# An attention and long-convolution kernel: the convolution kernel's spectrum from a table of matmuls instead of an expanded table and an FFT, and one order list for the whole program

## The chip, the cores and the metric

The kernel runs on one core of a Trainium2 chip. A core has five engines with an instruction queue each: TensorE (PE; the load of its weights is shown as PEld), VectorE (DVE), ScalarE (ACT), GpSimd (POOL) and SyncE (SP, which here only issues DMAs). Work passes from one to the other through semaphores. The metric is the device time of one execution in microseconds, lower is better.

## The reference, cut to what matters

```python
x = A_x                                        # bf16, 1 x 2048 x 640
g = sigmoid((x * gate_w).sum(-1))              # one gate for each position
a = attention(x, wqkv, wo)                     # 32 heads of 20, each position sees 8 positions, 2 apart
b = ssm(x, A, B, C, log_dt, Dskip)
out = g * a + (1 - g) * b

def ssm(u, ...):                               # 640 channels, 192 complex states each
    l = arange(2048).astype(bfloat16)
    P = exp(dt * A * l)                        # 640 x 192 x 2048, complex
    K = einsum("dn,dnl,dn->dl", C, P, dt * B).real
    y = irfft(rfft(pad(u, 4096)) * rfft(pad(K, 4096)))[:2048]     # causal convolution along the positions
    return y + u * Dskip
```

The positions `l` are rounded to bf16, so of 2048 positions only 641 are distinct: 0 to 256, then steps of 2, 4 and 8. The convolution kernel K has 641 different values for each channel, repeated over the positions that round to the same number.

## The kernel before

The host part of the program adds tasks with a name, an engine, dependences and buffer slots to a `Plan`; a list of numbers (`SEQ1`, later `SEQ2`) gives the order in which the tasks are emitted. The tasks of an engine run in that order. A letter behind a number says which of ScalarE (A) and VectorE (D) does an eviction that either could do. The data flows in these steps:

- **Start** (`Attn.loads`, `Attn.window`, `SSMParams.build`). x is loaded in four quarters and transposed on TensorE (tasks `turn`, line L200; evictions `tev`). The parameter chain, passes over 128x960 values on VectorE and ScalarE from `wr` (L582) to the last subtraction (L615), turns A, B, C and dt into pieces of phases and logarithms. They go to DRAM (`Sprm`) and come back as matmul weights (`L`, line L720).
- **Attention** (`Attn.plan_late`, `plan_core`). Projections of 512 positions (`late`, L291, evictions `lev`); products of q and k on VectorE (`prod`, L350); sums over a head on TensorE (L356); maximum (`mx`, L370) and normalisation (`at`, L391); products with v (`pv`, L419); sums (`gat`, L425) with evictions `oT`; output projection (`wo`, L443); gated result (`ga`) into DRAM (`gaS`).
- **Kernel values** (`KGen.plan`). Ten chunks of channels. In each, matmuls on `L` (L747) give arguments, ScalarE takes sines (L759) and exponentials (L761), VectorE multiplies them (`pt`, `qq`, L782 to L784) and TensorE sums over the states (`kmm`, L800, weights of 32 columns). The two factors span 32 positions in steps of 8 and 22 offsets; `fin` (L1214) copies a chunk's sums to `E`.
- **Expansion** (`KExpand`), after five chunks each. VectorE copies the entries of `E` to all 2048 positions (`X`, L846), the result goes to DRAM (`Kx`) and comes back with other rows (`kc`).
- **FFT of 4096 points as 32 x 64.** `first` does the first step (L1231) for K (`f1`, `fk`, from `kc`) and the input (`fu`, from `Usb`) in tasks of eight matmuls, with evictions of 128x1024 (L469 on ScalarE, L471 on VectorE).
- **Second list** (`fft_conv`). Eight blocks of frequencies. For K and the input, real and imaginary part, one task each (`fp`, L1008, PHI of 128 columns as weights, real and imaginary inputs as two accumulating matmuls), evicted on ScalarE (`sp_k`, `sp_u`, 128x1280); on VectorE the complex product (L1041, sums L1044) into `Y`. Then the inverse: first step (L1069, evictions `cp`), last step with psi as weights (`yp`, L1097), and the mix with the gated attention result `gaF` (L1103, L1106, L1110), stored from L1122 on. `PHI` (384 KB for each block), `psi` and `gaF` are loaded bit by bit, each behind a small copy that waits for an eviction.

The line that evicts a block of the spectrum, and the product, before:

```python
evict(nc, en, spec[nm, ro][:], fp[:, :, 0:320].rearrange("p f x -> p x f"))          # 128 x 320 x 4
nc.vector.tensor_tensor(t[o][:, 4*x0:4*x1], spec[i0][:, 4*x0:4*x1], spec[i1][:, 4*x0:4*x1], ALU.mult)
nc.vector.tensor_tensor(yv[:, ro, 4*x0:4*x1, 4*fb:4*fb + 4], t[f"ta{ro}"][...], t["tc"][...], (ALU.subtract, ALU.add)[ro])
```

Of the kernel before, what the change touches and what calls it, by code (L numbers as in the profile page):

```python
# [20 lines left out]
S = 2048  # L21
D = 640
# [14 lines left out]
def _attn_consts():  # L37
# [7 lines left out]
    for wp in range(W):  # L45
# [3 lines left out]

PLAN = dict(free=dict(P=4.0, A=4.2, D=4.7, S=16.0, G=16.0), phase=0.0, ms=-562.9, kg=3.6, wl=2678.4, look=0.3, ba=-39.4, bd=-694.1, grace=2227.4, p0=-605.9, p1=7.4,  # L50
            tx=[1831.6, 2062.6], txw=316.4, ql=-639.9, vl=-579.1, pw=39.8, el=-872.0, tl=303.3, vw=170.4, gate=1159.7,
            l=[985.4, 547.2, 222.2, 579.5, 238.7, 662.0, 1153.9, 985.5, 777.6, 1276.6, 963.9, 1335.9],
            a=[-383.8, 509.3, -1088.5, -67.5, 191.2, 725.6, 1205.9, 786.5], v=[1509.9, 971.2, 1675.0, 1085.1, 2426.4, 1181.7, 871.1, 1340.5],
            g=[102.8, 729.6, -565.5, -597.5, -1036.3, -403.5, 622.8, -317.4, -275.5, -968.3, -775.7],
            dl=[157.8, 67.2, 403.1, 10.3, -181.3, 324.5, 197.3, 230.9, 179.6, -259.4],
            kl=[-437.0, -232.8, -303.6, -188.9, -840.1, 140.8, -865.3, -73.8, -172.8, -518.6], Ll=2038.2, argl=332.8, xl=787.7, c0=5667.4, x0=-271.9, x1=332.2,
            f0=-509.9, f1=247.7, u0=1630.4, u1=60.1, off={0: 260.3, 9: 345.9, 27: 254.6, 47: 93.4, 96: -22.0, 105: -27.0, 107: 4.7, 131: -28.8, 140: -41.5,
            142: 18.2, 145: -3.0, 146: -3.7, 149: -9.3, 151: -10.5, 155: -2.9, 166: -1.8, 173: 5.1, 193: -12.8, 197: -5.4, 208: 10.3, 210: -36.0, 218: -30.6,
            1004: -8.8, 1022: -37.2, 1083: 6.1, 1089: 5.2, 1099: -2.5})


SEQ1 = """
8 0 2 3 1 6 4 14 13 5 7 26 27 9 10D 11D 18 12 74 76 28 75A 77A 78 79A 82 80 83D 15 17 23 81A 114 115D 120 94 56 121D 19 20 88 95A 104 37 21 116 105A 29 117A 84 100 89A
101A 85A 108 92 109A 93A 118 119A 22 229 24 34D 31 35D 39 36 42 25 90 110 98 230 86 111A 99A 32 106 43 16 30 38 33 107A 96 45 97A 40 146 147A 135 136A 122 87A 123A 57 46
58 41 44 62D 51D 231 52 53 47 60 61 102 103A 125 126A 129 91A 130A 48 112 113A 63 50 59 139 140A 64A 65A 154 232 152 222 155A 67 66 233 49 69 153A 54 68 70 55 71 72 127
234 137 128A 73 235 236 143 138A 223 144A 237 516 238 133 265 239 131 224 267 134A 240 241 132A 148 242 225 150 226 149A 243 151D 518 519 266 268 520 141 521 269 517 244
563 245 562 522 270 524 523 271 273 525 272 526 528 167 994 527 529 142D 124 221 228 145 264 227 156 530 532 274 178 531 533 301 168D 275 179D 534 536 535 537 186 276 538
540 175 187A 176D 303 539 541 542 544 180 277 278 184 543 545 279 181D 546 548 302 304 182 547 549 185A 305 307 550 552 306 157 309 551 553 183A 280 608 609 281 564 566
308 310 173 554 311 177 188 158A 565 567 568 570 555 312 159 569 174A 313 160A 571 314 161 572 574 171 162A 573 575 172A 556 337 315 339 165 576 578 338 340 169 559 557
558 577 579 170A 166A 341 342 580 582 581 583 343 345 163 584 586 344 346 210 164A 585 587 246 347 588 590 211A 589 591 199 348 200A 592 594 207 205 349 208A 373 600 375  # L70
206D 593 350 201 203 351 595 596 598 202A 597 599 560 374 376 610 612 249 204A 611 613 189 377 379 561 614 616 378 381 615 617 247 618 620 619 621 190A 601 380 382 622
624 623 625 191 248D 602 252 383 605 409 411 626 603 628 627 630 192A 629 631 197 198A 384 632 633 634 604 636 212 216 635 637 213D 606 638 640 217A 639 250 253 641 251A
642 644 646 607 648 254D 214 316 385 643 645 386 387 352 654 655 317 701 700 388 647 656 658 215A 657 659 195 660 662 661 193 663 651 196D 282 194A 664 666 410 255 665
667 256D 668 412 670 257 218 669 413 415 219D 258D 285 671 672 673 674 649 675 676 678 650 677 680 679 681 209 300 682 259 683 684 685 686 414 687 416 688 690 652 689 702
691 703 704 261 705 692 260D 417 653 445 694 706 708 707 709 262A 283 710 711 712 713 693 714 716 695 715 717 718 719 720 696 721 722 723 418 724 726 725 727 288 697 284D
419 286 289 728 420 447 698 730 755 756 353 263 729 287D 290D 732 699 738 421 731 733 291 734 736 422 735 737 757 758 759 739 761 740 423 318 743 292D 760 762 763 741 765
764 766 767 769 768 801 802 770 293 446 771 448 742 773 772 774 775 777 776 778 294A 744 779 781 780 782 295 783 784 449 451 745 793 785 787 786 789 788 790 791 450 792
452 803 805 297 296A 804 806 807 794 809 808 811 298A 810 812 319 813 320A 814 795 746 453 481 321 324 454 815 816 817 819 818 820 821 823 822 824 325 825 827 322 483 455
749 323D 798 326A 826 828 796 829 797 830 747 456 748A 457 831 832 833 327 834 458 835 836 750 839 459 837 424 848 847 389 299 751 894 460 893 799 849 220 336 838 851 482
850 852 800 328D 841 485 853 854 855 840 856 857 484 859 858 860 842 861 862 329 331 863 865 486 864 487 488 867 866 868 869 843 871 870 844 330D 873 333 872 874 332A 875  # L80
876 877 845 878 879 880 489 885 846 887 354 881 882 883 884 490 895 897 896 899 898 900 901 886 902 903 905 334A 904 906 355 907 909 908 910 888 911 912 913 914 491 357
356D 360 890 915 492 372 752 754 995 996 753 940 335 939 425 916 917 918 919 920 889 921 358 361 923 922 924 925 891 927 390 359D 926 362A 928 929 363 931 892 364D 393
933 941 930 365 943 942 493 944 945 932 367 947 946 366A 948 368A 949 369 951 391 370D 392D 396 950 952 953 934 935 955 394 954 956 957 958 371 997 408 998 999 1000 1001
# [10 lines left out]
103 112 117 114 122 119 104 116 118 123 124 120 125 121 126 134 127 128 135 129 137 136A 138 130 140 141 139D 143 142A 144 146 147 131 149 145A 132 150 152 148D 153 151A  # L94
155 156 133 158 154A 157D 159 161 162 160A 164 163D 165 167 168 166A 170 171 169D 173 172A 174 176 177 175D 179 178A 180 182 183 181D 185 184A 186 188 189 187D 191 190A
192 193D 194 197 195 201 198 204 202 209 196 211 205 210 216 199 200 212 203 219 223 206 217 226 213 207 208 220 224 215 232 214 218 227 225 221 222 233 228 236 234 235
231 230 229
""".split()


# [10 lines left out]
class Plan:  # L111
# [5 lines left out]
    def __init__(self, **pr):  # L117
        self.tasks, self.pr = [], pr
# [411 lines left out]
class SSMParams:  # L530
# [5 lines left out]
    def build(self, ctx, tc, pl, A_re, A_im, B_re, B_im, C_re, C_im, log_dt, gate_w, ident, gw_sb, pa, xl, wl):  # L536
# [17 lines left out]
        for w_ in wl:  # L554
            w_()
# [755 lines left out]
```

## Time and profile before

| | |
|---|---|
| median of 3 runs | 368.19 us (367.46 to 370.22) |
| span of the profiled execution | 365.8 us |
| TensorE, VectorE, ScalarE busy | 298.9, 310.5, 305.4 us |
| GpSimd busy | 72.7 us |
| DMA moved | 46.60 MB, mean 127 GB/s |
| VectorE's first parameter step begins | 5.37 us |
| first sine | 64.98 us |
| first and last copy of finished kernel values | 118.32 and 256.93 us |
| first last-step matmul | 347.69 us |

The profiled span is the time from the first to the last recorded work of one execution; the runs' times are 2 to 4 us above it. A row of a group reads: line, engine, operation, output and inputs, shapes, count, then busy time in us and mean ns of one instruction, then the idle time of the engine in front of them and what ended it. A row of the timeline reads: start, length, engine, line, operation, and how many instructions it joins. A row of windows gives, for each engine, the busy time in that stretch and the instructions.

### The profile page before, as it was taken

What the parts mean: (1) busy time and instruction counts of PE and PEld (TensorE: products, weight loads), DVE (VectorE), ACT (ScalarE), POOL (GpSimd) and SP (SyncE); (2) the same over time, 40 slices, a digit from 0 to 9 for tenths busy, and PEclk for the clock granted to TensorE, in tenths of its full rate; (3) what the DMA queues carried; (4) which work ended last, traced back from release to release, by engine and by line L of the source; (5) the groups of instructions that cost most, each with busy time, mean ns of one, the idle gap of its engine ahead of it and who ended that gap; (6) DMA issues with size and microseconds to landing.
All of it is one profiled execution on the core that took longest, in us unless ns stands there. A gap on an engine that the chain in (4) does not pass through costs nothing. (4 is left out here: it accounts for less than half of the span.)

```text
span 365.8 us, 12199 instructions
## 1 busy us (share of the span) xinstructions
PE 298.9 (82%) x5286; PEld 174.9 (48%) x5286; DVE 310.5 (85%) x407; ACT 305.4 (83%) x423; POOL 72.7 (20%) x113
## 2 busy tenths in 40 slices
PE   0199999939999989987887688899996799978770
PEld 0165454314444554454344334467663465557660
DVE  4899999817999999999999698999983469999972
ACT  1799997746999889999999789999994699988881
POOL 8930110300001100010021112165010023310032
PEclk9999999978999999999999659999998899999985
DMA  8941196541401421362157666559553149943037
GB/s 262 372 156 56 67 263 168 104 133 28 131 9 19 105 49 33 108 154 38 36 146 222 148 144 140 135 115 254 143 164 125 38 115 236 225 86 75 2 86 206
DMA packets 44041, 46.60 MB, mean 127 GB/s; under 512 B 24516, under 2 KB 38132, under 8 KB 43732
## 3 DMA queue, kind: packets, MB, share of 16 engines
q1 hardware_dynamic: 36116, 24.43, 25.6%
q0 software_dynamic: 5840, 20.55, 21.8%
q10 hardware_dynamic: 2032, 0.85, 0.9%
q8 instruction: 41, 0.67, 0.8%
q14 instruction: 12, 0.10, 0.1%
HBM read 31.31 MB, written 14.51 MB: 125 GB/s over the span
## 5 line engine op out<-in xcount | busy, mean ns | idle before, releaser
L291 PE MATMUL tb<-bufA 128*128 128x512 bf16 x300 | 75.7, 393 | 6.6 <-ACT prj L469 5.9
L759 ACT ACTIVATE big<-ar 128x608 bf16<-128x608 int16 x96 | 59.3, 685 | 8.2 <-PE ar L747 7.1
L747 PE MATMUL ar<-Rarg,L 64*128 64x304 bf16 (+1 forms) x480 | 55.5, 286 | 12.4 <-ACT big L759 4.3
L761 ACT ACTIVATE big<-ar 128x864 bf16<-128x864 f32 x60 | 49.5, 923 | 3.4 <-PE ar L747 3.0
L291 PEld LDWEIGHTS <-bufA 128*128 128x128 bf16 x300 | 33.0, 121 | 37.7 <-issue 16.5
L419 DVE TENSOR_TENSOR pv<-vc,asb 128x4096 bf16<-128x4096 bf16 (+1 forms) x24 | 46.1, 1930 | 1.5 <-PE tb L425 1.5
L747 PEld LDWEIGHTS <-L 64*128 64x128 bf16 x480 | 21.0, 95 | 47.5 <-issue 44.5
L1008 PEld LDWEIGHTS <-PHI 128*128 128x128 bf16 x288 | 26.8, 99 | 18.2 <-issue 9.2
L800 PE MATMUL kps<-qq,pt 128*32 128x22 bf16 (+1 forms) x2560 | 26.4, 176 | 3.8 <-issue 3.7
L443 PE MATMUL tb<-wo_sb,oT 128*128 128x320 bf16 x160 | 28.4, 315 | 0.5 <-issue 0.5
L800 PEld LDWEIGHTS <-pt 128*32 128x32 bf16 (+1 forms) x2560 | 22.5, 92 | 11.7 <-issue 9.0
L350 DVE TENSOR_TENSOR prod<-prj 128x2048 bf16<-128x2048 bf16 x20 | 23.9, 1221 | 0.6 <-POOL prj L311 0.4
L350 DVE TENSOR_TENSOR prod<-qk 128x2048 bf16<-128x2048 bf16 x20 | 23.9, 1221 | 0.0
L425 PE MATMUL tb<-pv,ind 128*64 128x512 bf16 (+1 forms) x192 | 22.4, 359 | 1.4 <-issue 1.4
L344 POOL DMA_DIRECT2D vc<-vS x16 | 11.5, 723 | 53.1 <-DVE pv L419 43.6
L469 ACT ACTIVATE prj<-tb 128x512 bf16<-128x512 f32 x27 | 16.0, 599 | 7.1 <-DMA vS<-prj 6.1
L784 DVE TENSOR_TENSOR qq<-big 128x1408 bf16<-128x1408 bf16 x24 | 21.3, 888 | 0.0
L1008 PE MATMUL fp<-big,PHI 128*128 128x320 bf16 x112 | 18.5, 311 | 1.9 <-ACT sp_u L469 1.2
L200 PE MATMUL ar<-ident,xn 128*128 128x128 bf16 x80 | 8.1, 264 | 14.4 <-DMA xn<-in_A_x_dram 14.0
L469 ACT ACTIVATE sp_u<-fp 128x1280 bf16<-128x1280 f32 x14 | 17.3, 1237 | 3.0 <-PE fp L1008 2.3
L1041 DVE TENSOR_TENSOR ta<-sp_u,sp_k 128x1280 bf16<-128x1280 bf16 (+1 forms) x18 | 13.4, 750 | 6.8 <-ACT sp_u L469 5.2
L1008 PE MATMUL fp<-bufA,PHI 128*128 128x320 bf16 x112 | 18.1, 306 | 1.2 <-DVE om L976 1.2
(173 smaller groups left out, 587.2 us busy)
## 6 DMA issues: line engine op xcount, KB each, us to landing
vc<-vS POOLq DMA_DIRECT2D x16, 327.5 KB, 6.0
PHI<-c_phi POOLq DMA_DIRECT2D x8, 384.0 KB, 6.3
Sprm<-pc SPq DMA_DIRECT2D x12, 240.0 KB, 5.2
L<-Sprm SPq DMA_DIRECT2D x80, 36.0 KB, 2.9
xn<-in_A_x_dram SPq DMA_DIRECT2D x4, 640.0 KB
gaS<-ga SPq DMA_DIRECT2D x8, 320.0 KB, 2.3
Usb<-in_A_x_dram POOLq DMA_DIRECT2D x8, 320.0 KB, 4.7
gaF<-gaS SPq DMA_DIRECT2D x8, 320.0 KB, 7.0
```

The costliest lines, as they stand in the source:

```text
L291: nc.tensor.matmul(ppf, self.wq[:, kt, which * D + e:(which + 1) * D:5], self.xT[:, c0 // 1024, kt, c0 % 1024:c0 % 1024 + SC], start=(kt = ...
L350: nc.vector.tensor_tensor(b[e][:], self.part(ch, 0)[:, e, o:o + C].unsqueeze(1).to_broadcast([128, W, C]), win(self.part(ch, 1)[:, e, :], ...
L419: nc.vector.tensor_tensor(b["pv", e][:, 0:2 * n], taps, aw, ALU.mult)
L425: nc.tensor.matmul(b["op", e][64 * a:64 * a + 64, 0:n, :], self.twin, b["pv", e][:, a:2 * n:2, w, :], start=(w == 0), stop=(w == HV - 1), ...
L443: nc.tensor.matmul(apf[:, :320], b["oT"][:, e, i * 128:(i + 1) * 128], wo_sb[:, e, hf * 320:(hf + 1) * 320], start=(e == 0), stop=(e == 4))
L469: nc.scalar.activation(o, i, ACT.Identity)
L747: nc.tensor.matmul(ar[:, g2, a0:a0 + ncol], L[rows, sb, gp, l0:l0 + 128], R[rows, c0:c0 + ncol], start=True, stop=True, tile_position=(64 ...
L759: nc.scalar.activation(dst[:, 2 * gp:2 * gp + 2, sub, :], ar[:].bitcast(I16)[:, :, 0:2 * SW:2], ACT.Sin, scale=SCL)
L761: nc.scalar.activation(dst[:, 2 * gp:2 * gp + 2].rearrange("p g s n -> p g (s n)"), ar[:, :, 0:2 * EW], ACT.Exp)
L784: nc.vector.tensor_tensor(qq[:], trg[:, :, KI:].rearrange("p a (v m) -> p a v m", v=2), exq[:, :, KI:].unsqueeze(2).to_broadcast([128, 32, ...
L800: nc.tensor.matmul(kps[32 * g:32 * g + 32, h, NM * ql:NM * ql + NM], pt[rows, k, v, :], qq[rows, k, v, :], start=(g not in started), stop= ...
L1008: nc.tensor.matmul(o.rearrange("p (c x) -> p c x", x=32), phis[fb][:, fl, kind, :], B[:, :, 2 * f1 + ri].rearrange("p c q g -> p c (q g)") ...
```

## The change

K is no longer expanded and transformed in steps. Its spectrum at 32 x 64 frequencies is linear in its 641 values, so it is a matmul with a constant table: 16 loads of 320 KB, used once for each of two channel parts (chunks 0 to 5, and 6 to 9). `KExpand`, `f1`, `fk`, their DRAM detour and the evictions `sp_k` go. New in their place:

- The offsets are 20 instead of 22, without position 0 (`MS`); sines are 576 wide instead of 608, exponentials 832 instead of 864, `qq` 1280 instead of 1408. Position 0 and Dskip, gathered on VectorE (`kred`, `kmix`), are added by one-row matmuls (`KSpec.lag0`).
- For each part (`KSpec.part`): two `move` tasks bring the values of `E` to other rows, two evictions put them into `KE`; 16 loads `wl` on SP (three buffers `W`); `ks` matmuls with weights of 64 columns, two side by side, of 192 (part 0, 32 tasks of 20) or 128 columns (part 1, 16 tasks of 40), and evictions `ske` straight into the spectrum `sk`.
- The input's first step (`fu`) is 20 tasks of 16 matmuls, that leave the real part in 64 rows and the imaginary part in the other 64. Its second step (`Conv.spectra`) is then one matmul of 128 rows and 64 columns for each output, two side by side: 256 matmuls instead of 288 for K and the input each of 320 columns or 160. `PHI` falls from eight loads of 384 KB to three loads, 1.05 MB in all.
- The complex product reads `sk` in runs of four values, 32 apart, and writes its result back into `sk`. The inverse of part 0 runs in the attention's PSUM buffers.
- One list `SEQ` holds all tasks, in a new order, and also chooses the DMA queue of some loads. VectorE's first task is `tev4`, behind TensorE's `turn8`, `turn3` and `turn4`. The projection weights are loaded behind the first parameters, the last two quarters of x behind these. More attention work stands before the first sine, less between it and the first finished chunk, more up to the tenth. Each table load waits for its buffer in SP's queue, in front of some of the attention's stores and of the loads of `L`. `gaF` and `psi` are issued on GpSimd, no longer behind small copies, after the last rows of `gaS` and the last `fu`.

The diff, cut to its core:

```diff
-MS = list(range(8)) + [258, 260, 262, 516, 772, 256, 512, 768, 1024, 1280, 1536, 1792, 2048, 2048]
+MS = list(range(1, 9)) + [258, 260, 262, 264, 516, 520, 772, 776, 1032, 1288, 1544, 1800]
-NTR, NEX = 5, 6
+NTR, NEX = 5, 5
+PARTS = ((0, 6), (6, 10))
-class KExpand:
...
+class KSpec:
+    def part(self, pl, p, f, pa, ps, ident, sk, opened, free):
+        for t in range(2):
+            def move(_, t=t, b=b):                      # 8 matmuls: rows of E to other rows
...
+            m = pl.add(f"move{p}{t}", "P", move, deps=[f], acq=["ar"])
+            kevs.append(pl.add(f"kev{p}{t}", "AD", ev, deps=[m], rel=[("ar", m)]))
+        nf = 2 if p == 0 else 4
+        for k in range(16):
+            fb, ro = k // 2, k % 2
+            def load(e, k=k, w=w):
+                w["t"] = self.W[self.nW % 3]
+                queue(nc, e).dma_start(w["t"][:].rearrange("p f m x -> p (f m x)"), self.w_d[k])
+            ld = pl.add(f"wl{p}{k}", "S", load, ..., acq=["W"])
+            for h in range(4 // nf):
+                def spec(_, ro=ro, h=h, w=w, b=b):
+                    for fl in range(nf):
+                        for m in range(M5):             # 5
+                            for c in range(2):
+                                nc.tensor.matmul(kp[64*c:64*c+64, fl], w["t"][:, nf*h+fl, m, :], self.KE[p][:, m, c]...,
+                                                 start=(m == 0), stop=(m == M5-1 and ro == 1), tile_position=(0, 64*c))
+                        if ro == 0:                     # position 0 and Dskip
+                            for c in range(2):
+                                nc.tensor.matmul(kp[64*c:64*c+64, fl], self.one[:], self.KD[...], start=False, stop=True, ...)
+                def ev(en, ...):
+                    evict(nc, en, sk[:, ro, 32*c0:32*c1, 4*fb+2*h:4*fb+2*h+2], b["v"].rearrange("p f x -> p x f"))
...
 class Conv:                                            # before: first, fft_conv
+    def first(...):
+                for q in range(8):
+                    k = 80 * c2 + 8 * c + q
+                    for ri in range(2):
+                        nc.tensor.matmul(bp[64*ri:64*ri+64, q//4, 128*(q%4):128*(q%4)+128], sf[:, k::160], self.F1c[:, 128*ri:128*ri+128],
+                                         start=True, stop=True, tile_position=(0, 64*ri))
+    def spectra(self, pl, p, pa, kg, ske):
+                    for fl in range(4):
+                        for c2 in range(2):
+                            nc.tensor.matmul(o[64*c2:64*c2+64]..., self.phi(kg.hold, fb)[:, fl, r, :],
+                                             self.Bu[:, c0:c1, c2, 4*fb+fl]..., start=True, stop=True, tile_position=(0, 64*c2))
+            def mul(_, fb=fb, b=b, k=0):
+                kk = [sk[:, r, 32*c0:32*c1, 4*fb:4*fb+4] for r in range(2)]
+                if k == 0:
+                    for r in range(2):
+                        nc.vector.tensor_tensor(t[r], u[0], kk[r], ALU.mult)
+                elif k == 1:
+                    nc.vector.tensor_tensor(u[0], u[1], kk[1], ALU.mult)
+                    nc.vector.tensor_tensor(u[1], u[1], kk[0], ALU.mult)
+                else:
+                    nc.vector.tensor_tensor(kk[0], t[0], u[0], ALU.subtract)
+                    nc.vector.tensor_tensor(kk[1], t[1], u[1], ALU.add)
...
 class SSMParams:                                       # order of the first loads
         load(nc.sync, "cre", C_re); load(nc.scalar, "bre", B_re)
         load(nc.sync, "cim", C_im); load(nc.scalar, "bim", B_im)
         xl[0]()
-        load(nc.sync, "aim", A_im)
+        load(nc.scalar, "aim", A_im)
         xl[1]()
+        for n, nm in enumerate(("cre", "bre", "cim", "bim")):
+            nc.gpsimd.tensor_copy(at.wq[:, 0, 2*n:2*n+2], t[nm][:, 0, 0:2])     # waits for the load
         for w_ in wl:
             w_()
-        load(nc.sync, "are", A_re)
         xl[2](); xl[3]()
+        load(nc.scalar, "are", A_re)
...
-    pl = Plan(seq=SEQ1, **PLAN)                        # and Plan(..., seq=SEQ2) in fft_conv
+    pl = Plan(SEQ)
```

More of the change, by code (lines that the diff above doesn't have):

```diff
@@ L62 @@
[L62 to L65, printed above, removed]
@@ L273, in plan_late @@
         self.freed, first = {}, {}
[L275 to L277 removed]
+        turns = [m_ for m_, e_ in self.xts]
         for sc in range(NSC):
@@ new lines, in gated_mix_kernel @@
+    kg.plan(pl, pa, pk, params + [prm.kd, kde], params, opened, fin)
+    kg.lastkmm = [t for t in pl.tasks if t.name in (f"kmm{NCH - 1}20", f"kmm{NCH - 1}00", f"kmm{NCH - 1}11")]
+    ub, cst = cv.loads(pl, kg, at, gate, opened)
+    cv.first(pl, ub, cst, pa, kg, opened)
+    cv.lastfp, cv.lastfe, cv.lastmul, cv.muls = None, [], None, {}
+    cv.freed = at.last + [at.gst]
+    for p in range(2):
+        cv.spectra(pl, p, pa, kg, ske[p])
+    psum = [t for t in pl.tasks if set(t.engs) <= set("PAD")]
@@ L1261 @@
+    cv.inverse(pl, pa, banks, psum)
+    cv.tail(pl, banks, at.last, [cv.lastfp])
+    pl.emit(tc)
 @with_exitstack
```

1090 lines of the change are left out of this document (536 added, 554 removed).

## The prediction

> **What bounds the kernel now.** I read first the page's span and busy shares, then the window view cut at the stages of the work, then the timeline at their borders, then the groups.
>
> ```profile
> span 365.8 us, 12199 instructions
> PE 298.9 (82%) x5286; PEld 174.9 (48%) x5286; DVE 310.5 (85%) x407; ACT 305.4 (83%) x423; POOL 72.7 (20%) x113
> ```
>
> No engine stands out over the span: three lie within 12 us, all above 80%. A share of the whole cannot say what a change is worth, so the cuts are: start to the first sine, to the first finished chunk of kernel values, to the tenth, to the first last-step matmul, and the tail (the row 257 to 347.7 is split at 291).
>
> ```profile
> core 0: us, PE busy (x) PEld busy (x) DVE busy (x) ACT busy (x) POOL busy (x), PEclk, DMA share, GB/s
> 0.00:20.00 20.00, 3.17 (x26) 2.62 (x27) 13.63 (x19) 9.64 (x11) 18.40 (x29) 1.00 0.94 317
> 0.00:65.00 65.00, 47.25 (x352) 26.98 (x353) 55.91 (x67) 51.42 (x69) 23.47 (x37) 1.00 0.61 190
> 65.00:118.30 53.30, 46.87 (x567) 21.14 (x567) 41.94 (x52) 41.00 (x63) 5.09 (x8) 0.94 0.30 71
> 118.30:257.00 138.70, 120.44 (x3196) 66.81 (x3194) 130.63 (x180) 129.50 (x192) 26.03 (x38) 0.95 0.51 122
> 257.00:291.00 34.00, 27.90 (x327) 18.71 (x326) 23.26 (x30) 24.65 (x35) 1.80 (x3) 0.93 0.39 122
> 291.00:347.70 56.70, 49.45 (x602) 35.02 (x600) 49.51 (x63) 49.85 (x47) 10.67 (x17) 0.98 0.51 119
> 300.00:320.00 20.00, 18.95 (x125) 11.93 (x123) 18.48 (x24) 18.64 (x16) 7.15 (x11) 1.00 1.00 235
> 347.70:365.80 18.10, 6.95 (x256) 6.25 (x256) 9.29 (x18) 9.01 (x21) 5.64 (x10) 0.69 0.58 147
> ```
>
> VectorE sets the long middle stage (130.63 of 138.70, a share of 0.942). After it, TensorE is busiest at 77.35 of 90.70, only 0.853: that stage has 13 us in which nobody works flat out. At the start VectorE is the busiest.
>
> ```profile
> 5.37 1.16 DVE L582 TENSOR_TENSOR wr<-cre,bre 128x960 f32<-128x960 bf16 x1 [1.44 <-DMA cre<-in_B_C_re_dram]
> ...
> 17.34 1.46 PE L200 MATMUL ar<-ident,xn 128*128 128x128 bf16 x12 [1.96 <-DMA xn<-in_A_x_dram]
> ...
> 53.55 1.16 DVE L615 TENSOR_TENSOR s<-at,pc 128x960 f32<-128x960 f32 x1
> ...
> 64.98 3.53 ACT L759 ACTIVATE big<-ar 128x608 bf16<-128x608 int16 x6
> ...
> 256.93 0.53 DVE L1214 CAST E<-kps 128x352 bf16<-128x352 f32 x1 [0.94 <-PE kps L800]
> ```
>
> VectorE runs from 5.37 on; its last step of the parameter chain ends at 54.71, and the first sine follows 10.27 us later.
>
> **The change, stage by stage.** Each sum starts from a window of before and adds the difference in instructions, at row durations.
>
> ```profile
> L350 DVE TENSOR_TENSOR prod<-qk 128x2048 bf16<-128x2048 bf16 x20 | 23.9, 1221 | 0.0
> L419 DVE TENSOR_TENSOR pv<-vc,asb 128x4096 bf16<-128x4096 bf16 x16 | 36.5, 2285 | 1.5 <-PE tb L425 1.5
> L391 DVE TENSOR_TENSOR at<-at,rs 128x512 bf16<-128x512 bf16 x8 | 5.5, 692 | 0.3
> L370 DVE TENSOR_REDUCE mx<-lg 128x64 f32<-128x512 f32 x8 | 5.5, 685 | 0.0
> L471 DVE CAST bufA<-bp 128x1024 bf16<-128x1024 f32 x5 | 6.1, 1225 | 7.4 <-PE bp L1231 7.2
> L471 DVE CAST oT<-tb 128x512 bf16<-128x512 f32 x11 | 7.6, 687 | 0.9 <-PE tb L425 0.6 <-issue 0.3
> L846 DVE COPY X<-E 128x80 bf16<-128x80 bf16 (+5 forms) x16 | 3.3, 285 | 0.0
> L784 DVE TENSOR_TENSOR qq<-big 128x1408 bf16<-128x1408 bf16 x24 | 21.3, 888 | 0.0
> L469 ACT ACTIVATE qk<-tb 128x512 bf16<-128x512 f32 x18 | 10.6, 601 | 0.6 <-PE tb L291 0.5
> L761 ACT ACTIVATE big<-ar 128x864 bf16<-128x864 f32 x60 | 49.5, 923 | 3.4 <-PE ar L747 3.0
> L759 ACT ACTIVATE big<-ar 128x608 bf16<-128x608 int16 x96 | 59.3, 685 | 8.2 <-PE ar L747 7.1
> ```
>
> *Start to first sine.* The new list opens VectorE's queue with the eviction of a transposed block of x, and TensorE's list puts transposes of the last quarters of x in front of it. Parameters, x and the projection weights are 6.55 MB; at the 317 GB/s of the first row they are in by 20.7 us, and with a group of transposes (1.46) VectorE begins near 22 instead of 5.37. All that stands behind, the parameter chain with it, is late by that. From its start to the chain's end it took 49.34; the new list puts four more products (4.9) and one more maximum and normalisation (1.4) before that point; the gathering of the lag-0 value comes in and two linear steps go to ScalarE, which I let cancel. 22 + 55.6 + 10.3 = 87.9, against 65.0: a loss of 23.
>
> *To the first finished chunk.* The products done early are missing here: 14 fewer, 17.1 of VectorE's 41.9. ScalarE loses 13 evictions (7.8) and 3 exponentials (2.8), gains one sine and two evictions (1.9), and its sines and exponentials are 32 columns narrower (about 27 ns each by the two rows' 238 ns for 256 columns, for 38 of them 1.0): 41.0 - 9.7 = 31.3, now the largest. At the share 0.942: 33.2, against 53.3.
>
> *To the tenth chunk.* Here the removed work pays for what was put off: VectorE gains 9 products (11.0), 2 value products (4.6), two each of maximum and normalisation (2.8) and 2 first-step evictions (2.5). It loses eight attention evictions against two gate ones (4.1 at 687), one half's spreading of the table (half of 3.3, 1.7), and 26 narrower products (128 columns, some 67 ns each, 1.7). 130.6 + 13.4 = 144.0; over 0.942 that is 152.9, against 138.7. ScalarE gains 17 evictions of 384 (0.5 by the row of 512) and other evictions, about 10 in all, and stays under it.
>
> ```profile
> 262.64 0.94 PE L1231 MATMUL bp<-F1c,Usb 64*128 64x128 bf16 x16
> 263.51 1.05 PE L425 MATMUL tb<-pv,ind 128*64 128x512 bf16 x8
> ...
> 264.97 0.63 PE L425 MATMUL tb<-pv,ind 128*64 128x256 bf16 x8
> ...
> 298.25 1.25 PE L1008 MATMUL fp<-bufA,PHI 128*128 128x320 bf16 x8
> L1008 PE MATMUL fp<-bufA,PHI 128*128 128x320 bf16 x112 | 18.1, 306 | 1.2 <-DVE om L976 1.2
> L1008 PE MATMUL fp<-big,PHI 128*128 128x320 bf16 x112 | 18.5, 311 | 1.9 <-ACT sp_u L469 1.2
> L291 PE MATMUL tb<-bufA 128*128 128x512 bf16 x300 | 75.7, 393 | 6.6 <-ACT prj L469 5.9
> 245.93 0.65 PE L800 MATMUL kps<-qq,pt 128*32 128x22 bf16 x64
> ```
>
> *The table of matmuls.* Its price is the least known. Columns alone: 134 ns for 320 columns (1.25 for eight, less some 0.18 for the pipeline) is 0.42 ns a column, so a pair of column tiles, side by side, costs 80 for 192 columns and, with a little for its loads, 60 for 128. There are 352 pairs of each: 49 us. The nearest rows with 64-column weights are L425's: pairs of 512 and 256 columns, about 217 and 118 ns, give 93 and 69 on their line: 57 us. A flat 118 a pair is the upper bound, 83. I take 49, nearer the row of many loads (64 small matmuls with 64 loads in 0.65, some 30 ns for four side by side).
>
> A rule of the Trainium skill speaks against this edit: "TensorEngine Tiling (Array Packing)", Restrictions, says column tiling switches Fast Weight Load off, and "TensorE: Matmul & The Clock Gate", LDWEIGHTS, gives a load its columns over 1.2 in nanoseconds. By it, as an estimate, two loads of 64 follow each other in 107 ns and 704 pairs are 75 us, 26 more. The four loads in 30 ns do not fit loads one behind the other, so I do not follow it in the sum.
>
> ```profile
> L1041 DVE TENSOR_TENSOR ta<-sp_u,sp_k 128x1280 bf16<-128x1280 bf16 x14 | 11.6, 825 | 6.7 <-ACT sp_u L469 5.2 <-ACT sp_k L469 0.4
> L1044 DVE TENSOR_TENSOR Y<-ta,tc 128x1280 bf16<-128x1280 bf16 x14 | 11.5, 822 | 0.2
> L1041 DVE TENSOR_TENSOR ta<-sp_u,sp_k 128x640 bf16<-128x640 bf16 x4 | 1.9, 487 | 0.1
> PHI<-c_phi POOLq DMA_DIRECT2D x8, 384.0 KB, 6.3
> gaF<-gaS SPq DMA_DIRECT2D x8, 320.0 KB, 7.0
> ```
>
> *To the first last-step matmul.* TensorE loses 41.8 of second step (36.6, and 64 half-wide ones at half price) for 128 pairs, 9.0; the other half's first step (80 matmuls at 59 ns, 4.7), six output projections (five at 252 x 320/512, 4.7) and three groups of L425 (2.7). It gains 15 table tasks of part 0 (11 pairs of 80: 13.2) and 16 of part 1 (22 pairs of 60: 21.1): 77.35 - 10.6 = 66.8. VectorE: the complex product is now 48 instructions of 768 and 48 of 512 (555 and 420 on the line through 825 and 487) for 42 and 12: 46.8 for 40.5, +6.3; 19 of the new evictions (384 to 768 values, 0.65 to 0.95 between the casts' 687 for 512 and 1225 for 1024), +13.9; minus 11 evictions of 1225 (13.5), four value products (8.1), the spreading and small ones (2.4): 72.8 - 3.8 = 69.0. ScalarE gives up 36 evictions of up to 1280 columns for 36 of at most 768, and falls below both. Dense, the stage is 69.0; at 0.942, 73.2. I take 70.5: the table's way through DRAM and back is gone, and so are the waits of the first step (7.4 in the cast's row). The tail is kept, 18.1.
>
> *Transfers.* 32 table loads of 320 KB come in on SP, 10.5 MB. One that waits for its buffer holds up the attention stores and the next chunk's arguments behind it on SP. The nearest, of 384 and 320 KB, land in 6.3 and 7.0; with three buffers one can land every 2.3, under the 4.3 per load that the two parts' 140 us allow. I cost them at nothing, hidden by the middle stage's products. On the Pool's queue the gate input and the last-step weights are no longer paced one by one behind evictions: they are issued in a bunch once the last attention rows are stored, beside the second half of the table. If the cover goes, rival (d) has the price.
>
> *Sum.* 87.9 + 33.2 + 152.9 + 70.5 + 18.1 = 362.6, against the profiled 365.8; the median, 368.19, lies 2.4 above the profiled span. Forecast: **365.0**, inside the 1% that a measurement of this kernel can tell from no change (364.5 to 371.9), at its fast edge.
>
> **Rivals.** (a) The idle of the stages goes, as the one list lets late attention fill both sides of the tenth chunk: 31.3, 144.0 and 69.0 in place of 33.2, 152.9 and 70.5 give 352.7. For it: in the last stage only two engines stay near the bound, where now three do (77.4, 72.8 and 74.5); against: 0.942 is what the written-out order of before reached in its longest stage.
> (b) TensorE becomes the bound of the middle stage. It gains 17 table tasks (15.0), eight first-step tasks' worth net of those removed (4.5), six projections of five (7.6): 120.4 + 27.1 = 147.5. Its best stretch above is 0.95, its share now 0.87: 155.3 to 169.5, halfway 162.4, giving 374.5. It decides from a share under 0.965.
> (c) Slower: the weight path limits the table, so that the 64-column pairs cost halfway to the flat 118. Middle: TensorE 151.0, at 0.95 159.0 (+6.1); last stage 66.8 + 13.4, with the same allowance 82.0 (+11.5): 382.6. At the full 118 it would be about 400. It decides once a pair costs over 85 ns; L425's rows speak for it, L800's against.
> (d) The table's second half meets the gate input and last-step weights, 9.96 MB in the last stage. At the 235 GB/s of the busy stretch, 42 us, hidden; at the 122 that the stage moved on average, 81.6: 376.1.
> (e) The products read the spectrum in runs of four, 64 bytes apart; at half rate 32 instructions of 768 and 32 of 512 cost 21.4 more (0.52 ns an element): 90.4 for 69.0, giving 386.9. L1044, which writes runs of four as fast as L1041, speaks against it.
>
> **How the numbers follow.** Forecast .42, its own range 358 to 371 (faster .22, same .18, slower .02); (a) .21 (faster); (b) .13 (same .04, slower .09); (c) .11 (slower); (d) .07 (same .02, slower .05); (e) .06 (slower). Faster .43, same .24, slower .33. The range reaches down past (a), where the start also loses its idle share of 0.06 (3.4) and a little of the sum errs, to 346, and up past (c) to 386; under 2 in 10 is left out.
>
> **What would show it.** Right: VectorE's first instruction after 20 us; first sine at 85 to 90; first finished chunk near 121, tenth near 274; VectorE busiest from there to the tenth at 0.94; pairs of the table 60 to 80 ns apart. Wrong: a sine before 80 (the start is hidden), TensorE above VectorE in the middle stage, table matmuls over 100 ns apart, products over 600 ns, or idle time ended by a table load.

## The result, and the profile after

The changed kernel takes 417.34 us (median of 4 runs, 417.03 to 418.52) against 369.21 for the kernel before: 1.132 times as long (95% interval 1.126 to 1.138). Forecast were 365.0, in a range of 346 to 386: wrong in sign and outside the range. The profiled execution has a span of 415.5 us. A few executions of a kernel ran over 1.5% longer than its fastest; the times and ratios of the runs below leave these out.

The page of the changed kernel, span and busy shares:

```profile
span 415.5 us, 15009 instructions
PE 348.9 (84%) x6687; PEld 212.5 (51%) x6687; DVE 308.0 (74%) x433; ACT 291.9 (70%) x442; POOL 52.3 (13%) x94
```

VectorE and ScalarE have a little less to do than before (310.5 and 305.4), TensorE has 50 us more (298.9). The window view, cut at the same events as before, with the stage from the first to the tenth chunk also shown in two halves (the sixth chunk ends near 208). The cuts here are the ends of the two copies of finished values; before and in the runs below they are their starts, by which the changed kernel's stages end at 125.5 and 300.5 and its last stage is 97.7:

```profile
core 0: us, PE busy (x) PEld busy (x) DVE busy (x) ACT busy (x) POOL busy (x), PEclk, DMA share, GB/s
0.00:91.20 91.20, 61.84 (x408) 33.72 (x409) 61.82 (x76) 57.77 (x81) 27.15 (x52) 0.99 0.53 156
91.20:125.90 34.70, 28.70 (x437) 12.25 (x436) 25.87 (x30) 25.85 (x39) 0.58 (x1) 0.82 0.44 103
125.90:300.90 175.00, 165.42 (x3806) 95.29 (x3803) 145.32 (x185) 147.67 (x232) 12.24 (x20) 0.98 0.44 98
300.90:398.20 97.30, 87.28 (x1786) 66.64 (x1785) 65.85 (x126) 51.77 (x73) 6.66 (x11) 0.95 0.47 125
398.20:415.50 17.30, 5.70 (x256) 4.64 (x255) 9.16 (x18) 8.88 (x21) 5.66 (x10) 0.76 0.60 154
208.00:300.90 92.90, 87.32 (x1914) 54.50 (x1907) 67.46 (x81) 67.62 (x106) 4.98 (x8) 0.96 0.54 122
125.90:208.00 82.10, 78.10 (x1903) 40.80 (x1901) 77.86 (x105) 80.05 (x127) 7.26 (x13) 1.00 0.32 71
```

| us | start to first sine | to first chunk | to tenth | to last step | tail | span |
|---|---|---|---|---|---|---|
| before | 65.0 | 53.3 | 138.7 | 90.7 | 18.1 | 365.8 |
| forecast | 87.9 | 33.2 | 152.9 | 70.5 | 18.1 | 362.6 |
| after | 91.2 | 34.7 | 175.0 | 97.3 | 17.3 | 415.5 |

The first two stages and the tail came out within 3.3 us. Most of the miss of 52.9 lies in two places: 22.1 between the first and the tenth chunk, 26.8 after it. There TensorE is busy for 0.95 and 0.90 of the time, and from the sixth chunk to the last step for 174.6 of 190.2 us, while VectorE has 133.3 and ScalarE 119.4: TensorE is now the busiest engine by far. Its new work, in groups (L923 the table, L927 the one-row matmuls that add position 0, L1100 the complex product on VectorE):

```profile
L923 PE MATMUL tb<-KE,W 128*64 128x192 bf16 x640 | 36.3, 252 | 0.0
L923 PE MATMUL tb<-KE,W 128*64 128x128 bf16 x640 | 27.0, 230 | 6.7 <-DMA W<-c_spec 6.7
L927 PE MATMUL tb<-KD,one 1*64 1x192 bf16 x64 | 15.7, 487 | 0.0
L927 PE MATMUL tb<-KD,one 1*64 1x128 bf16 x64 | 12.3, 380 | 0.0
L1100 DVE TENSOR_TENSOR tbx<-tbx,bufA 128x768 bf16<-128x768 bf16 x16 | 8.3, 553 | 0.9 <-ACT bufA L459 0.9
L1100 DVE TENSOR_TENSOR tbx<-tbx,bufA 128x512 bf16<-128x512 bf16 x16 | 6.1, 418 | 0.1
```

128 one-row matmuls are busy for 27.9 us, nearly a third of the table's 90.9. The timeline of TensorE shows the price of each kind as the step to the next row's start:

```profile
300.63 0.49 PE L927 MATMUL tb<-KD,one 1*64 1x192 bf16 x2
301.05 0.60 PE L923 MATMUL tb<-KE,W 128*64 128x192 bf16 x10
301.58 0.49 PE L927 MATMUL tb<-KD,one 1*64 1x192 bf16 x2
302.00 1.02 PE L923 MATMUL tb<-KE,W 128*64 128x192 bf16 x20
302.85 0.50 PE L1073 MATMUL ar<-big,L 128*64 128x192 bf16 x8
...
354.17 2.35 PE L923 MATMUL tb<-KE,W 128*64 128x128 bf16 x40 [4.54 <-DMA W<-c_spec]
...
361.54 1.31 PE L923 MATMUL tb<-KE,W 128*64 128x128 bf16 x40
362.68 1.06 PE L1073 MATMUL ar<-big,L 128*64 128x128 bf16 x32
```

Twenty table matmuls of 192 columns take 0.85, 85 ns a pair; forty of 128 columns take 1.14, 57 a pair: my 80 and 60. But two one-row matmuls of 192 columns take 0.42, where a pair of the table takes 0.085. The ten table matmuls behind them take 0.53 (301.05 to 301.58), 0.1 more than ten of the twenty from 302.00 on. The row at 354.17 belongs to the clock, below.

### The profile page after: what moved, and what is told of

It reads as the page before. It is cut to its first block, busy times and chain, and to the rows that moved or that the text cites. A ratio compares the mean times of both kernels' runs of the same rounds, so it can differ in the third digit from the quotient of the medians.

```text
span 415.5 us, 15009 instructions
## 1 busy us (share of the span) xinstructions
PE 348.9 (84%) x6687; PEld 212.5 (51%) x6687; DVE 308.0 (74%) x433; ACT 291.9 (70%) x442; POOL 52.3 (13%) x94
## 3 DMA queue, kind: packets, MB, share of 16 engines
q10 hardware_dynamic: 3200, 1.31, 1.3%
## 5 line engine op out<-in xcount | busy, mean ns | idle before, releaser
L775 ACT ACTIVATE big<-ar 128x576 bf16<-128x576 int16 x120 | 71.9, 653 | 20.2 <-PE ar L763 19.2
L923 PE MATMUL tb<-KE,W 128*64 128x192 bf16 (+1 forms) x1280 | 63.0, 241 | 6.7 <-DMA W<-c_spec 6.7
L763 PE MATMUL ar<-Rarg,L 64*128 64x288 bf16 (+1 forms) x480 | 55.0, 282 | 11.2 <-DMA L<-Sprm 3.0
L923 PEld LDWEIGHTS <-W 128*64 128x64 bf16 x1280 | 47.4, 113 | 21.6 <-issue 12.3
L777 ACT ACTIVATE big<-ar 128x832 bf16<-128x832 f32 x60 | 49.2, 880 | 3.0 <-PE ar L763 2.5
L279 PEld LDWEIGHTS <-bufA 128*128 128x128 bf16 x300 | 33.2, 121 | 34.1 <-issue 12.6
L812 PE MATMUL kps<-tbx 128*32 128x20 bf16 (+1 forms) x2560 | 26.2, 175 | 4.9 <-issue 4.9
L812 PEld LDWEIGHTS <-tbx 128*32 128x32 bf16 (+1 forms) x2560 | 22.5, 91 | 11.3 <-issue 7.9
L927 PE MATMUL tb<-KD,one 1*64 1x192 bf16 (+1 forms) x128 | 27.9, 433 | 0.0
L796 DVE TENSOR_TENSOR tbx<-big 128x1280 bf16<-128x1280 bf16 x30 | 24.5, 817 | 0.0
L337 DVE TENSOR_TENSOR prod<-uga 128x2048 bf16<-128x2048 bf16 x20 | 24.1, 1219 | 0.0
```

The lines of the kernel that those rows point to most:

```text
L279: nc.tensor.matmul(ppf, self.wq[:, kt, which * D + e:(which + 1) * D:5], self.xT[:, c0 // 1024, kt, c0 % 1024:c0 % 1024 + SC], start=(kt = ...
L337: nc.vector.tensor_tensor(b[e][:], self.part(ch, 0)[:, e, o:o + C].unsqueeze(1).to_broadcast([128, W, C]), win(self.part(ch, 1)[:, e, :], ...
L763: nc.tensor.matmul(ar[:, g2, a0:a0 + ncol], L[rows, sb, gp, l0:l0 + 128], R[rows, c0:c0 + ncol], start=True, stop=True, tile_position=(64 ...
L775: nc.scalar.activation(dst[:, 2 * gp:2 * gp + 2, sub, :], ar[:].bitcast(I16)[:, :, 0:2 * SW:2], ACT.Sin, scale=SCL)
L777: nc.scalar.activation(dst[:, 2 * gp:2 * gp + 2].rearrange("p g s n -> p g (s n)"), ar[:, :, 0:2 * EW], ACT.Exp)
L796: nc.vector.tensor_tensor(qq[:, :, :, :], trg[:, :, KI:].rearrange("p a (v m) -> p a v m", v=2), exq[:, :, KI:].unsqueeze(2).to_broadcast( ...
```

## The experiments

All ran beside the kernel before on the same chip; ratios are to that, so that they can be set beside the changed kernel's 1.132. A hundredth of the ratio is 3.7 us.

**Position 0 read in one run.** The values are loaded as (half, channel, group) instead of (group, half, channel):

```diff
-self.KD[:, :, c, 8 * c0:8 * c1].rearrange("p g x -> p x g")     # step of 160 values
+self.KR[:, c, 8 * c0:8 * c1].rearrange("p x g -> p (x g)")
```

> The 128 one-row matmuls that add position 0 read their 192 or 128 values in one run instead of with a step of 160 values (the tiny load of these values is written in the other order); nothing else changes. Theory A: the stepped read sets their price (0.42 and 0.31 us for two, where two table matmuls of the same widths take 0.083 and 0.06), and TensorE sets the time from the first finished chunk on: TensorE gives up about 19 us and the kernel 15 to 19, to 398 to 402. Rival B: a matmul of one row is slow by itself: the time stays at 417, within 2, and the pairs stay at 0.42 and 0.31. Rival C: the price falls as in A, but TensorE is not the bound and the time falls by less than 8.

411.98 us, ratio 1.117 (1.110 to 1.124): 5 us. Its one-row groups and its last stage:

```profile
L931 PE MATMUL tb<-KR,one 1*64 1x192 bf16 x64 | 8.8, 271 | 0.0
L931 PE MATMUL tb<-KR,one 1*64 1x128 bf16 x64 | 8.0, 247 | 0.0
...
297.60:393.50 95.90, 84.85 (x1794) 70.92 (x1789) 66.30 (x127) 52.45 (x74) 6.68 (x11) 0.89 0.49 127
```

27.9 us of one-row matmuls have become 16.8: the step of 160 values costs, as A said. The rest of their price stays, so B holds in part. And of the 11 us only 5 reach the time: C is nearer than A. The granted clock of the last stage is 0.89 here, 0.95 in the changed kernel; over the whole kernel this execution had the lowest clock of its four, 0.925 against 0.937 to 0.950.

**No one-row matmuls** (`if ro == 0:` never taken).

> The one-row matmuls are left out (position 0 and Dskip are then missing from the spectrum). Theory A: about 23 us less on TensorE, 394 to 398, and at most 5 below the contiguous variant. Rival B: this alone falls, by 20 or more, while the contiguous variant stays. Rival C: less than 10.

401.94 us, ratio 1.088 (1.078 to 1.097): 16 us. The profiled spans differ by 14.5, and 12.3 of it is the last stage (97.7 to 85.4):

```profile
297.80:383.20 85.40, 69.53 (x1704) 63.37 (x1701) 65.91 (x127) 51.87 (x74) 6.68 (x11) 0.94 0.53 143
```

TensorE gave up 23.7 (325.2 for 348.9), some two thirds of which reached the time. The one-row matmuls are thus the largest single cause found, a third of the loss; the saving in A was too high. In the last stage TensorE now has 69.5 us of work, close to the 66.8 that I had forecast, and still the stage lasts 85.4.

**The start.** The eviction at the head of VectorE's queue goes to ScalarE (`85D` becomes `85A` in the list).

> The eviction that opens VectorE's queue goes to ScalarE, so that VectorE begins with the parameter chain as soon as the parameters are loaded, about 5 us instead of 25. Theory A (TensorE bounds the kernel from the arrival of x on): the first sine comes up to 10 us earlier, but the time falls by less than 4, 413 to 417. Rival: the late chain is on the path, and the time falls by 10 to 20, to 397 to 407.

415.82 us, ratio 1.128 (1.121 to 1.135): within A, but not yet a test. VectorE began early and then stood still behind ScalarE, whose queue also opens with a transposed block (waits view of this run):

```profile
DVE s L594 <- ACT s L596: 17.6, 1, 17.6
```

So the next run puts the chain's first steps ahead on both queues.

```diff
-1130S 92 1119G 93A 82 83A 84 85D 0 1 4 94 88 89A ...
+0 1 4 15 3 9 11 2 12A 8 6 13D 10 14 ... 1130S 92 1119G 93A 82 83A 84 85D 94 88 89A ...
```

> Giving one eviction to ScalarE did little because ScalarE's own queue then stood at a transposed block of x and VectorE waited for it (17.6 us). Here the first 15 VectorE steps of the parameter chain, and ScalarE's steps between them, stand ahead of all transposed blocks on both queues; the rest of the order is unchanged. If the late start is on the path, the first sine comes 10 to 15 us earlier than 91 and the time falls by as much, to 402 to 407. If TensorE bounds the kernel from the arrival of x on, the first sine comes earlier but the time falls by 6 at most.

416.81 us, ratio 1.126 (1.118 to 1.134): the second of the two. The first sine came 2 us earlier, the first chunk 4.5 us, and the tenth at the same time as in the changed kernel (300.5). Its window from 20 us to the first sine:

```profile
20.00:89.20 69.20, 59.29 (x400) 31.67 (x407) 50.32 (x58) 51.52 (x71) 10.28 (x27) 0.96 0.43 119
```

TensorE had waited 11.6 us for x before (waits view) and is busy for 59 of these 69 us, more than VectorE and ScalarE: this fits TensorE as the bound from the arrival of x on. Third, the projection weights were made to wait for x:

```diff
-for n, nm in enumerate(("cre", "bre", "cim", "bim")):
-    nc.gpsimd.tensor_copy(at.wq[:, 0, 2*n:2*n+2], t[nm][:, 0, 0:2])
+for n in range(4):
+    nc.gpsimd.tensor_copy(at.wq[:, 0, 2*n:2*n+2], at.xn[n // 2][:, 4 * (n % 2), 0:2])
```

> On top of the parameter chain ahead of the transposed blocks, the projection weights wait for the quarters of x instead of for the first parameters, so that x has the transfers for itself. TensorE begins at about 14 instead of 20.4 us. Theory (TensorE is the bound from the arrival of x on): the time falls by 5 to 8 against the chain alone, to 407 to 412. Rival (the start is hidden by what follows): less than 2.

418.46 us, ratio 1.133 (1.121 to 1.145): nothing. But the edit did not do what it was for. TensorE's first transposes began at 19.14, not at 14 (timeline of this run), so what an early x would bring is still open:

```profile
19.14 0.61 PE L149 MATMUL ar<-ident,uga 128*128 128x128 bf16 x4 [10.38 <-DMA uga<-in_A_x_dram]
```

**The table loaded once** (`if self.nW <= 3:` ahead of the load).

> Only the first three of the 32 table loads are issued; the matmuls use what lies in the three buffers (the spectrum is then wrong from the fourth on). Theory: the waits of TensorE for table loads in the last stage, 7 us in three waits, go, and with them 6 to 9 of the time: 408 to 411. Rival: these waits cover others (evictions, the inverse's buffers), and the time falls by less than 3.

415.07 us, ratio 1.125 (1.118 to 1.132): 2 us, the rival. The waits for loads went, but the last stage fell only from 97.7 to 96.6, with TensorE busier than before:

```profile
299.90:396.50 96.60, 90.12 (x1798) 69.21 (x1793) 66.24 (x127) 52.25 (x74) 6.68 (x11) 0.93 0.24 55
```

**A fifth of the table's matmuls** (`for m in range(1)`, no one-row matmuls).

> Of the five matmuls that add up an output of the table only the first is issued, and no one-row matmuls: TensorE loses 0.8 x (320 x 0.083 + 320 x 0.06) = 36.6 us and 23 for the one-row ones, all after the sixth chunk (the spectrum is then incomplete); loads and evictions stay. Theory (TensorE is the bound from the sixth chunk to the last step, 174.6 of 190 us): VectorE, with 133 us of work there, becomes the bound, and the time falls by 38 to 50, to 367 to 379. Rival (the order and its waits, evictions or loads are the bound): it falls by less than 25, to over 392.

393.01 us, ratio 1.062 (1.056 to 1.068): 25.6 us, little over half of what the theory said, and at the edge of its rival (25 us, 392). Windows of this run:

```profile
208.00:293.10 85.10, 70.81 (x1654) 43.20 (x1640) 67.12 (x82) 66.42 (x106) 5.38 (x8) 0.92 0.60 133
293.10:375.30 82.20, 54.45 (x952) 45.27 (x948) 65.70 (x127) 51.83 (x74) 6.67 (x11) 0.77 0.55 147
...
325.00:345.00 20.00, 7.68 (x123) 6.13 (x121) 12.85 (x27) 4.98 (x8) 3.25 (x6) 0.50 1.04 232
```

With TensorE at 297 us, the amount of before, no engine is full in either stage. From 325 to 345 all engines are slack and the transfers run at 232 GB/s: table loads and gate input, behind the last-step weights issued from 317 on. That is the meeting of my rival (d), which the full TensorE had covered.

**The second part alone.**

> The same for the table's second part alone (15.4 and 10 us of TensorE, nearly all after the tenth chunk); the first part is whole. Theory: the last stage falls from 97.7 to 75 to 81, the stages before stay within 2, the time is 395 to 401. Rival: the waits for table loads and the evictions keep the last stage over 90.

410.41 us, ratio 1.110 (1.103 to 1.117): 8 us for the 25 taken away. The last stage is 88.3 for 97.7, between theory and rival:

```profile
303.20:391.50 88.30, 66.03 (x1220) 52.73 (x1218) 65.92 (x127) 52.17 (x74) 6.67 (x11) 0.85 0.52 137
```

**A fifth, and loaded once.**

> The table's matmuls cut to a fifth as before, and only the first three table loads issued. Loading once gave 2 us alone and the fifth 24. Theory (two limits lie over each other in the last stage: with TensorE relieved, the 5 MB of table loads beside 4.7 MB of gate input and last-step weights are what is waited for): together 7 to 12 more than the fifth alone, 381 to 386, all of it in the last stage. Rival: within 3 of 393.

387.21 us, ratio 1.049 (1.040 to 1.058): 5 us more than the fifth alone, between the theory (7 to 12) and its rival (3). The last stage is down by 10, close to the 70.5 that I had forecast for it, but in this execution it begins 3 us later:

```profile
296.10:368.40 72.30, 49.63 (x951) 41.64 (x946) 65.17 (x127) 51.52 (x74) 6.68 (x11) 0.91 0.30 72
```

**The other way round: the kernel before with its second FFT step issued twice** (`for fl in (0, 0, 1, 1, 2, 2, 3, 3)`).

> The kernel before, with each matmul of the second FFT step issued twice (same result): about 35 us more of TensorE work after the tenth chunk, where TensorE is busy for 77 of 91 us, and nothing else changed. Theory (extra TensorE work in the late stages is enough to make the loss): the last stage grows by 25 to 35, to 394 to 404 in all. Rival (the new order is what costs, not the work): it grows by less than 12.

395.9 us, ratio 1.070 (1.058 to 1.082). The last stage of before, and of this run:

```profile
257.00:347.70 90.70, 77.34 (x928) 53.72 (x926) 72.76 (x93) 74.50 (x82) 12.47 (x20) 0.96 0.47 120
...
261.10:379.50 118.40, 108.32 (x1216) 80.24 (x1215) 73.27 (x93) 75.78 (x82) 12.64 (x20) 0.97 0.33 91
```

31 us more of TensorE, 27.7 more in the stage, 26 in the whole by the ratio: where TensorE is the busiest, extra work on it costs nearly its whole length, in the old order too.

**The loads of the input's rows.** The changed kernel issues them in a burst. Timeline of SP's and GpSimd's queues and of VectorE in the changed kernel:

```profile
205.69 4.68 POOL L1004 DMA_DIRECT2D uga<-in_A_x_dram  x6 [32.59 <-DVE tbx L794]
206.76 0.53 SPq L1004 DMA_DIRECT2D uga<-in_A_x_dram  x1
207.51 7.68 SPq L331 DMA_DIRECT2D vc<-vS  x2
225.79 2.29 DVE L406 TENSOR_TENSOR pv<-vc,asb 128x4096 bf16<-128x4096 bf16 x1 [7.93 <-DMA aS<-at]
```

SP needs 7.7 us to issue the two halves of a value load behind them, and VectorE then waits 7.9. The row loads were put on GpSimd's queue, each behind the one before:

```diff
+if n:
+    nc.gpsimd.tensor_copy(self.pace[32*g0:32*g0+32, :], self.Usb[32*g0:32*g0+32, 32*h0, 0:2])
```

> Nothing but the eight loads of the input's rows for the first FFT step changes: as in the kernel before, all are on GpSimd's queue and each waits, by a small copy, for the one before it. In the changed kernel seven of them are issued in 10 us at 206 and VectorE then waits 7.9 us for the softmax rows on their way through DRAM. Theory (from the sixth chunk TensorE is the bound, so VectorE's wait is covered): the wait shrinks, but the time falls by 3 at most. Rival (the wait is on the path): it falls by 6 to 9, to 408 to 411.

Ratio 1.133 (1.120 to 1.145), no change: the theory's place. But the waits view of this run says that the stall was not taken away either: another load now comes late, a value load that stands behind the paced ones on GpSimd's queue.

```profile
DVE pv L406 <- DMA vc<-vS: 6.4, 1, 6.4
```

> The changed kernel with the row loads replaced by the fill, and nothing else: the whole table and its loads. Theory (TensorE covers the stall): 0 to 4 less than 417. Rival: 7 or more less.

418.50 us, ratio 1.138 (1.130 to 1.146): no gain. VectorE's wait of 7.9 is gone, but the fill held one of its small steps for 5.90 instead of 0.19 us, so whether the whole table covers the stall stays open:

```profile
208.52 5.90 DVE L360 TENSOR_SCALAR hi<-mx 128x64 bf16<-128x64 f32 x1
```

Then all four together:

> All four together: a fifth of the table's matmuls and no one-row ones, table loaded once, rows paced, parameter chain and x first. TensorE's work is then that of the kernel before. If the four account for the loss, the time is 366 to 374, that of the kernel before. Rival (the order of the list is itself worse, whatever the work): it stays over 380.

384.44 us, ratio 1.042 (1.034 to 1.051): 3 us less than without pacing and start, which is inside the noise; the rival. The stall is still there, at the products with v (waits view). The view names no releaser; a value load for these products stands behind the paced loads on GpSimd's queue:

```profile
POOL uga L973 <- issue: 34.6, 3, 34.0
DVE pv L370 <- issue: 7.1, 1, 7.1
```

> A fifth of the table, loaded once, with the parameter chain and x first, and the eight row loads of the input's first step replaced by one fill with zeros on GpSimd (the input's part of the convolution is then zero). If the stall beside the row loads is the rest of the loss, the 384 with paced rows falls to 372 to 377, all of it between the sixth and the tenth chunk. Rival (it is covered by something else, the order of the list in general): within 3 of 384.

382.40 us, ratio 1.042 (1.036 to 1.048). This run does not decide either, for the same reason:

```profile
206.62 5.90 DVE L324 TENSOR_SCALAR hi<-mx 128x64 bf16<-128x64 f32 x1
```

Next, that value load is moved from GpSimd's queue to SP's (`447G` becomes `447S`):

> The run with all four (384), with that one value load moved from GpSimd's queue, where it waits behind the paced rows, to SP. If this queue order makes the stall of 7 us at the products with v, the time falls to 375 to 379. Rival: the wait only moves on (to SP's queue or to the softmax rows): within 3 of 384.

376.9 us, ratio 1.026 (1.016 to 1.035): 6 us by the ratio, as expected, though the intervals of the two runs touch and the profiled spans differ by 3.4 only (380.3 and 376.9). VectorE still waits 4.8 at these products, now for softmax rows, so the rival holds in part. The halves of the middle stage in this run, and its last stage:

```profile
123.10:205.00 81.90, 76.63 (x1826) 40.54 (x1834) 77.40 (x105) 79.74 (x126) 5.75 (x11) 1.00 0.30 70
205.00:287.20 82.20, 70.15 (x1662) 43.47 (x1660) 67.68 (x82) 66.54 (x107) 13.86 (x16) 0.94 0.51 106
287.20:359.40 72.20, 49.04 (x952) 41.03 (x950) 65.11 (x127) 51.53 (x74) 6.64 (x11) 0.91 0.30 72
```

**Nothing left out**: position 0 in one run, chain and x first, rows paced, value load moved.

> Nothing left out: position 0 read in one run, parameter chain and x first, rows paced, and the value load that stood behind the paced rows on GpSimd's queue moved to SP. The single effects were 5 for the first and 0 to 3 for the others; with TensorE still the bound 405 to 411. Rival (the stall was on the path as well): 395 to 403.

404.76 us, ratio 1.102 (1.094 to 1.111): 11 us better than the changed kernel, just under the range that I had expected, and still a tenth slower than before. Position 0 alone gave 5 of the 11. The other 5 are more than the start runs and the pacing gave singly; no run with the whole table says which of the three edits brought them. No version of the table that ran here beats the kernel before.

## Why the prediction was wrong, step by step

**What held.** VectorE began at 24.9 (22 forecast), the first sine came at 91.2 (87.9), the first chunk at 125.9 (121.1), the tail took 17.3 (18.1). VectorE's middle stage had 145.3 us of work (144.0). Table pairs cost 85 and 57 ns (80 and 60). The products took 553 and 418 ns (555 and 420), so rival (e) is out. The prediction's estimate of 107 ns for two 64-column loads one behind the other, worked out from the Trainium skill's load rule ("TensorE: Matmul & The Clock Gate", LDWEIGHTS), does not hold for these pairs. Two of the signs of being wrong came: TensorE above VectorE in the middle stage, and 6.7 us of idle TensorE that a table load ended.

**The step that failed first: "352 pairs of each".** I counted 64 pairs of one-row matmuls as table pairs. They cost 0.42 and 0.31 us: 32 x 0.34 + 32 x 0.25 = 19 us too little, 12 of it on the last stage's sum of 66.8, and some 0.1 on top for the table matmuls behind each pair. Without them TensorE has 69.5 us there instead of 87.3: but for them the sum was nearly right. What I had not asked is how their operand lies in memory: a step of 160 values. A rule of the Trainium skill that the prediction left aside is in "SBUF — State Buffer", in the note on cachelines under Door 1: accesses that change to a new 16-byte line each time pay. The run with the values in one piece agrees (27.9 to 16.8 us); what makes the remaining 0.20 us a pair is open.

**The bound of the middle stage.** I divided VectorE's work by one share, 0.942, over 153 us. The stage has two halves, and the table can start only when the sixth chunk is done. In the first half all three engines are over 0.94, ScalarE at 0.975 (I gave ScalarE "about 10" more; it has 18, of which two evictions into `KE` at 2.3 us each). In the second, TensorE is at 0.94 and VectorE at 0.73. A stage's sum by its busiest engine is too low where the engine changes within it. Rival (b) named TensorE, but its sum, 147.5, missed the one-row matmuls (9.3 us) and attention work that moved here, above all 39 more matmuls of the projections of 512 positions (20.1 us for 10.0): 165.4 were measured.

**The last stage: 70.5 against 97.3.** Two limits lie on top of each other. TensorE at 87.3 is the first: with 69.5 (no one-row matmuls) the stage lasts 85.4, with 54.5 (a fifth of the table) 82.2. The second are the transfers that I "cost at nothing": with a fifth of the table and loaded once, 72.3. Taken away alone, the loads gave 2 us, taken away behind TensorE, 10 of the stage.

**Moved pacing.** I named gate input and last-step weights, not the input's rows. What their burst costs with the whole table is open: pacing alone and the fill alone brought no gain, but each put another hold-up of VectorE (6.4 and 5.9 us) in the place of the 7.9. With TensorE relieved, moving the value load out from behind the paced rows is worth 3 (by the profiled spans) to 6 us.

**What was shown, and what is open.** Of the 49 us, 26 go with TensorE's work for the table (16 of them with the one-row matmuls) and 5 with the loads. Start, pacing and the value load's queue together took another 9; how these split is not shown, since pacing had itself put paced rows in front of that value load. The last version, with four fifths of the table and most loads left out, is still 2.6% (1.6 to 3.5) above the kernel before with less TensorE work than it (290.1 us). By stage, what is left lies between the first and the tenth chunk: 164.1 us for 138.7 before, while the last stage takes 72.2 for 90.7. Every engine has more to do there than before (VectorE 145.1 for 130.6, with no more work in all), as the new list moved work in from the stages beside it. The two halves last 82 each, the first dense, the second not held by any engine. Why the second half is not shorter, and whether another order would bring it back, no run shows.

**One reason why cuts may give back less than their length.** In the changed kernel the 40 matmuls after the wait of 4.54 us took 2.35, the same 40 later 1.31. The granted clock of the last stage went from 0.95 to 0.85 with the second part cut and 0.77 with a fifth, 0.50 in the stretch from 325 to 345 where table matmuls wait 2 to 3 us at a time: in these runs idle gaps are followed by slow matmuls. It is not less work as such: without one-row matmuls the clock was 0.94, and with a fifth loaded once, without the waits for loads, 0.91. How much of the time this cost is not measured. The Trainium skill's page "TensorE: Matmul & The Clock Gate", Part 1, says that about 3.4 us without work halve the clock and that work brings it back; the 4.54 us and the factor of 1.8 agree. The waits of 2 to 3 us in the stretch above are each shorter than that; what kept the clock down between them no run separates.

## What to carry to other kernels

Price every matmul that a change adds by what it reads, not by its columns alone: 128 of 1408 table matmuls, with one row each and a stepped operand, cost nearly a third of the table. Cut a stage where the new work becomes possible, and ask of each part which engine is busiest there; work that can start only late piles up on the engine that is then full. And where one limit is taken away and little comes back, look for the next one under it before calling the first harmless: here the loads behind TensorE's work.

## What was not expected of the hardware

- Two one-row matmuls of 192 columns, read with a step of 320 bytes, take 0.42 us, in one piece 0.20; a pair with 128 rows in one piece takes 0.085.
- ScalarE's eviction of 960 values into `KE`, written with steps, takes 2.34 us, one of 1024 values into the transposed x takes 1.02 (no run has the step alone changed):

```profile
208.45 2.34 ACT L459 ACTIVATE KE<-ar 128x960 bf16<-128x960 f32 x1
```

- With seven row loads under way, SP needs 7.7 us to issue the two halves of a value load, 7.07 of it for one; the median half takes 0.6.
- A fill on GpSimd held one VectorE step of 128x64 for 5.90 instead of 0.19 us, in both runs that had it.
